# Attention weights of a windowed transformer block: the turn moved from TensorE products to 32x32 block transposes on VectorE, with all instruction orders replaced

## The chip, the cores and the metric

The kernel runs on one core of one Trainium2 chip. The metric is the device time of one execution in microseconds (us), from several runs; beside it there is one profiled execution, whose span (first to last instruction) and trace the text reads. TensorE is called PE below (PEld is its weight load), VectorE DVE, ScalarE ACT, GpSimd POOL, and SyncE SP. SP issues the transfers (DMAs).

## The reference

A transformer block with adaptive layer norm on 2048 tokens of width 512: attention over a dilated window, and a gated feed-forward network.

```python
# x: (1, 2048, 512), H = 32 heads of 16, W = 8 positions, dilation 2, F = 1792
mod = silu(c) @ w_mod                      # sa, ca, ga, sb, cb, gb
h = layernorm(x) * (1 + ca) + sa
q, k, v = h @ wqkv
idx = pos[:, None] - 2 * arange(8)         # token t sees t, t-2, ... t-14
logits = einsum('bhsd,bhswd->bhsw', q, k[idx]) * 16 ** -0.5
logits = where(idx >= 0, logits, -1e9)
attn = softmax(logits)
x = x + ga * (einsum('bhsw,bhswd->bhsd', attn, v[idx]) @ wo)
h = layernorm(x) * (1 + cb) + sb
x = x + gb * ((silu(h @ w1) * (h @ w3)) @ w2)
```

## The kernel before

**Tiles.** The tokens are 16 tiles of 128. Everything from the input x to the output of a tile stays in SBUF, but for v, which is stored to DRAM and read back with the window's shifts. Tiles are grouped differently in each stage: the first layer norm and the projections go by groups 0-1, 2-3, 4-7, 8-11, 12-15; logits, softmax and the weights' turn by pairs of tiles (eight pairs, each using one PSUM bank of 512 columns); the feed-forward network by the groups 0-1, 2-3, 4-7, 8-11, 12-13, 14-15.

**The attention of a tile.** `logits` (L731) multiplies q and the shifted keys on DVE, eight positions at once, into a tile `pq` of 128x4096 (`prod`, L742). There features lie on partitions. `red` (L752) sums over the 16 features of each head with TensorE: the PE array is used as four column groups of 32 (a "tiled" product), each group of 32 PSUM partitions takes a quarter of the tile's tokens, and its 32 partitions are the heads. So the PSUM bank holds, on partition (group, head), eight positions by 32 tokens for each of two tiles. For tile 0 a product of a constant `before` (made by POOL at the start, L395 to L397) adds the mask of positions ahead of the sequence (L749). `shift` takes the maximum over the positions (L764) and subtracts it (L769); `exps` is on ACT (L782); `softmax` sums (L794), takes the reciprocal (L796) and multiplies (L797), all on DVE, into `attn`, whose partitions are (group, head) and whose columns are (token, position).

**The turn.** The values need the weights with the tokens and positions on partitions: partition = position and token of a group of 16, columns = (one of eight token groups, head). `turn` makes that by four PE transposes a pair of tiles (L807) into a PSUM bank `ps_at`, which ACT copies to the SBUF tile `al` (L811).

**The values.** `values` (L815) loads a tile's shifted v with four transfers (L820), multiplies them with `al` on DVE (L827, 128x4096), sums over the positions on PE (`acc2`, L855, tiled), evicts on ACT (L861), turns the result with a transposing DMA, multiplies with wo on PE (L867) and adds to x on DVE (L871), which also yields the row sums of the second layer norm.

**Second layer norm and feed-forward.** `ln_sums` (L582): mean on POOL (L586), squares on ACT (L590), two further POOL steps (L596 and the next) and the bias (L599), normalization on ACT (L601). `ln_T` (L609) turns the result with transposing DMAs for the groups from 4-7 on and scales it on ACT (L621). `ffn_unit` (L876) does one of 14 units of 128 hidden features: w1 on PE, silu on ACT (L889), w3 on PE (both L883), product on DVE (L892). `ffn_w2` (L899) sums over the units (L921; L909 for the last two tiles), and `store` adds x on DVE (L931) and stores. Feed-forward units of earlier tiles run between the attention of later ones.

**What sets the order.** Each call of `p.op` records one operation of one engine (`p.dma` one transfer). `ORDER` (L980) is a list of all 1118 operations' numbers; each engine takes its own operations in that order, and within an engine nothing overtakes. `SLOTS` says which buffer or PSUM bank each value uses. `synchronize` (L165) then adds the semaphore waits. All transfers but one small one are issued by SP in the same list. The late weight parts (w1, w3 in four parts each, loads 14 to 21, and w2 in four, loads 22 to 25) have places in it like everything else.

## Time and profile before

| | |
|---|---|
| three runs | 239.23, 239.90, 240.03 us; median 239.9 |
| profiled execution, span | 237.7 us, TensorE clock 1.000 |
| PE busy | 229.7 us (97%) |
| DVE busy | 179.4 us (75%) |
| ACT busy | 138.5 us (58%) |
| POOL busy | 29.2 us (12%) |
| instructions | 4535 |

The page gives the span of the profiled execution and no time of its own beyond that; the median of the runs is 2.2 us above the span. Rows of the groups have the line, the engine, the operation, out<-in, shape and count, then the busy time and the mean of one record in ns, then the idle time of the engine just before, with what ended it. Rows of the timeline have the start, the duration, engine, line, operation and count; brackets hold a wait and what released it. Rows of the stretches have the window, its length, then for PE, PEld, DVE, ACT and POOL the busy us (and number of instructions), then the granted clock, the share of DMA and GB/s. Rows of the waits have the us waited, how often, and the longest.

### The profile page before, as it was taken

How to read it: one execution, taken by the hardware profiler on the slowest of the kernel's cores; microseconds unless marked ns; L12 is line 12 of the kernel's file. 1: busy time of each engine (PE TensorE's matmuls, PEld its weight loads, DVE VectorE, ACT ScalarE, POOL GpSimd, SP SyncE). 2: the span in 40 equal slices, each digit the busy share in tenths (PEclk: the TensorE clock that was granted, in tenths of full speed). 3: DMA queues.
4: the chain of work that ended last, by engine and by line, in shares of the span. 5: the costliest groups of instructions: out<-in, count | busy, mean ns of one | idle time of the engine just before them, and what ended most of it. 6: DMA issues, size and time to landing. Idle time of an engine off the chain costs nothing.

```text
span 237.7 us, 4535 instructions
## 1 busy us (share of the span) xinstructions
PE 229.7 (97%) x1781; PEld 136.2 (57%) x1806; DVE 179.4 (75%) x279; ACT 138.5 (58%) x267; POOL 29.2 (12%) x66
## 2 busy tenths in 40 slices
PE   7999999999999998999999999999999999999995
PEld 4776454445588674664444444444475457485774
DVE  5699999999999989999999999682654403434433
ACT  2289577999978744985865594837473405040300
POOL 4434100013002000240002520012010000000000
PEclk9999999999999999999999999999999999999999
DMA  6999999999999999897981693642203000000202
GB/s 216 372 337 322 158 237 299 208 269 283 353 200 270 243 249 199 173 260 177 247 234 47 182 234 72 154 132 46 67 19 91 3 0 0 6 19 0 70 0 88
DMA packets 46317, 38.85 MB, mean 163 GB/s; under 512 B 21704, under 2 KB 37080, under 8 KB 46296
## 3 DMA queue, kind: packets, MB, share of 16 engines
q1 hardware_dynamic: 46288, 38.56, 66.9%
q8 instruction: 14, 0.23, 0.4%
q14 instruction: 7, 0.06, 0.1%
q10 hardware_dynamic: 8, 0.00, 0.0%
HBM read 29.62 MB, written 4.21 MB: 142 GB/s over the span
## 4 chain that ended last, share of the span: by engine, by line
PE 74%; DMA 8%; DVE 8%; SPq 4%; ACT 3%; issue 2%; ACTq 0%; DVEq 0%
PE pall L883 38%; PE pall L921 18%; DMA sb_x<-in_A_x_dram 5%; PE pall L867 5%; SPq L124 4%; PE pall L691 4%; DMA sb_vsh<-v_scratch_dram 3%; PE pall L909 3%; PE pall L855 2%; PE pall L752 2%; PE pall L711 2%; DVE sb_vsh L827 2%; DVE sb_pq L742 2%; DVE sb_hh L892 1%; ACT sb_h L621 1%
## 5 line engine op out<-in xcount | busy, mean ns | idle before, releaser
L883 PE MATMUL pall<-sb_h,sb_w 128*128 128x256 bf16 (+1 forms) x664 | 101.9, 307 | 1.8 <-DVE sb_hh L892 0.9
L883 PEld LDWEIGHTS pall<-sb_h,sb_w 128*128 128x128 bf16 x672 | 64.8, 98 | 37.2 <-issue 2.8
L889 ACT ACTIVATE sb_sg<-pall 128x256 bf16<-128x256 f32 (+1 forms) x84 | 35.6, 453 | 54.1 <-PE pall L883 53.0
L892 DVE TENSOR_TENSOR sb_hh<-sb_sg,pall 128x256 bf16<-128x256 bf16 (+1 forms) x84 | 39.9, 505 | 34.8 <-PE pall L883 32.7
L921 PE MATMUL pall<-sb_w,sb_hh 128*128 128x512 bf16 x190 | 44.0, 379 | 0.3
L742 DVE TENSOR_TENSOR sb_pq<-sb_q,sb_kT 128x4096 bf16<-128x4096 bf16 x16 | 36.3, 2282 | 0.0
L921 PEld LDWEIGHTS pall<-sb_w,sb_hh 128*128 128x128 bf16 x196 | 19.0, 98 | 21.6 <-DVE sb_hh L892 0.4
L691 PE MATMUL pall<-sb_h,sb_wqkv 128*128 128x512 bf16 (+1 forms) x154 | 30.2, 335 | 0.5 <-issue 0.2
L827 DVE TENSOR_TENSOR sb_vsh<-sb_vsh,sb_al 128x4096 bf16<-128x4096 bf16 x12 | 27.3, 2287 | 2.1 <-DMA sb_vsh<-v_scratch_dram 2.1
L621 ACT ACTIVATE sb_h<-sb_h,sb_modc 128x512 bf16<-128x512 bf16 (+1 forms) x24 | 16.5, 743 | 10.1 <-DMA sb_h<-sb_xn 10.1
L691 PEld LDWEIGHTS pall<-sb_h,sb_wqkv 128*128 128x128 bf16 x160 | 14.7, 98 | 11.8 <-ACT sb_ac L861 0.4
L931 DVE TENSOR_TENSOR sb_o<-pall,sb_x 128x512 bf16<-128x512 f32 (+1 forms) x18 | 11.1, 625 | 10.5 <-PE pall L921 6.8
L711 PE MATMUL pall<-sb_wqkv,sb_h 128*128 128x512 bf16 x62 | 15.5, 379 | 0.2
L867 PE MATMUL pall<-sb_wo,sb_ot 128*128 128x512 bf16 x61 | 15.3, 379 | 0.3 <-issue 0.2
L586 POOL TENSOR_SCALAR sb_nm<-sb_sx 128x2 f32<-128x2 f32 x8 | 1.7, 218 | 105.2 <-DVE sb_x L871 105.1
L644 ACT ACTIVATE sb_h<-pall,sb_modc 128x256 bf16<-128x256 bf16 (+1 forms) x18 | 9.9, 612 | 7.5 <-DVE sb_modc L509 6.5
L861 ACT ACTIVATE sb_ac<-pall 128x512 bf16<-128x512 f32 x16 | 9.5, 595 | 7.2 <-PE pall L855 7.1
L601 ACT ACTIVATE sb_xn<-sb_x,sb_nb,sb_rs 128x512 bf16<-128x512 bf16 x16 | 12.4, 806 | 0.7 <-POOL sb_nb L599 0.6
L871 DVE SCALAR_TENSOR_TENSOR sb_x<-pall,sb_x 128x512 bf16<-128x512 f32 x16 | 10.9, 686 | 1.5 <-PE pall L867 1.3
L590 ACT ACTIVATE sb_xn<-sb_x,sb_nm 128x512 bf16<-128x512 bf16 x16 | 11.4, 714 | 0.7 <-POOL sb_nm L586 0.7
L721 ACT ACTIVATE sb_v<-pall 128x512 bf16<-128x512 f32 x16 | 9.5, 600 | 2.8 <-PE pall L711 2.8
L555 DVE BATCH_NORM_STATS2 sb_st<-sb_x 128x6 f32<-128x512 bf16 x16 | 10.6, 680 | 0.8 <-DMA sb_x<-in_A_x_dram 0.7
(87 smaller groups left out, 208.3 us busy)
## 6 DMA issues: line engine op xcount, KB each, us to landing
sb_vsh<-v_scratch_dram SPq DMA_DIRECT2D x48, 256.0 KB, 5.5
sb_vshx<-v_scratch_dram SPq DMA_DIRECT2D x16, 256.0 KB, 4.6
sb_w<-in_B_w_dram SPq DMA_DIRECT2D x6, 512.0 KB, 7.9
sb_w<-in_B_w_dram SPq DMA_DIRECT2D x6, 384.0 KB, 5.4
v_scratch_dram<-sb_v SPq DMA_DIRECT2D x16, 128.0 KB, 6.4
out_dram<-sb_o SPq DMA_DIRECT2D x14, 128.0 KB, 1.8
sb_wqkv<-in_A_wqkv_dram SPq DMA_DIRECT2D x6, 256.0 KB, 6.3
sb_x<-in_A_x_dram SPq DMA_DIRECT2D x4, 256.0 KB, 6.4
```

Of the source, the lines that this page charges most:

```text
L590: p.op("act", lambda e, vn=vn, T=T: e.activation(vn.at[:], x_sb[:, T, :], ACT.Square, bias=nm[:, T, :], accum_out=var[:, T, :]), c_act(512 ...
L601: p.op("act", lambda e, vn=vn, T=T: e.activation(vn.at[:], x_sb[:, T, :], ACT.Identity, bias=nb[:, T, :], scale=rs[:, NT + T, :]), c_act(5 ...
L621: return e.activation(vh.at[:, ft, 0:n * P], vh.at[:, ft, 0:n * P], ACT.Identity, bias=modc[:, 8 * which + ft:8 * which + ft + 1], scale=m ...
L691: ins = e.matmul(bank(vp)[:, j * n:(j + 1) * n], wqkv[:, t, col:col + P], vh.at[:, t, 0:n], start=(t == ORDER[0] and j == 0), stop=(t == O ...
L711: ins = e.matmul(bank(vp), vh.at[:, t, tt * P:(tt + 1) * P], wqkv[:, t, 2 * D:3 * D], start=(t == ORDER[0]), stop=(t == ORDER[-1]))
L742: return e.tensor_tensor(vp.at[:], in0, in1, ALU.mult)
L827: return e.tensor_tensor(v_w, v_w, a_w, ALU.mult)
L867: ins = e.matmul(bank(vy), vt.at[:, ft, :], wo[:, ft, :], start=(ft == 0), stop=(ft == KT - 1))
L883: ins = e.matmul(bank(vp)[:, 0:n], wt[:, t, fi * P:(fi + 1) * P], vh.at[:, t, 0:n], start=(t == 0), stop=(t == KT - 1))
L889: p.op("act", lambda e: e.activation(vt.at[:, 0:n], bank(vgp)[:, 0:n], ACT.Silu), c_act(n), k, r=[vgp], w=[vt], table="silu")
L892: p.op("dve", lambda e: e.tensor_tensor(vh_.at[:, 0:n], vt.at[:, 0:n], bank(vup)[:, 0:n], ALU.mult), c_dve(n), k, r=[vt, vup], w=[vh_])
L921: ins = e.matmul(bank(vz), vhh[fi].at[:, tt * P:(tt + 1) * P], w2[:, fi, :], start=(fi == 0), stop=(fi == NF - 1))
```

## The change

The change has three parts.

The turn: `attn` is turned by two DVE block transposes a pair of tiles, which transpose each 32x32 block by itself (32 partitions of one column group by 32 columns), straight into `al` in SBUF. The four PE transposes, the PSUM bank `ps_at` and the ACT copy are gone. Each of the two instructions takes 256 elements of every partition.

The tokens: a block transpose stays inside its 32 partitions. So that each lands where the values need it, column group q of `red` now takes tokens 8q to 8q+7 of every 32 (four runs of eight, where it took two interleaved rows of 16 from one 32). The mask of tile 0 then concerns two column groups in place of one; `before` is made by two selects and added by two products.

The orders: `ORDER` and `SLOTS` are replaced as a whole. There are 1111 operations: PE 376 (before 384), DVE 271 (263), ACT 233 (241), POOL 63 (62), SP 168 (168).

```diff
-    before = sb([P, W, 2, 16], bf, "before")
+    before = sb([P, 2, W, 4, 8], bf, "before")
...
-    p.op("pool", lambda e: e.affine_select(out=before[:], in_=before[:], compare_op=ALU.is_ge, fill=BEFORE, base=0,
-                                           pattern=[[-DIL, W], [1, 2], [2, 16]], channel_multiplier=0), 400, k, w=[vbefore])
+    for q in range(2):
+        p.op("pool", lambda e, q=q: e.affine_select(out=before[:, q], in_=before[:, q], compare_op=ALU.is_ge, fill=BEFORE, base=8 * q,
+                                                    pattern=[[-DIL, W], [32, 4], [1, 8]], channel_multiplier=0), 400, k, w=[vbefore])
...
                 if T == 0:
-                    e.matmul(PALL[0:32, c0:c0 + W * 32], ones[:, 0:32], before[:], start=True, stop=False, tile_position=(0, 0))
+                    for q in range(2):
+                        e.matmul(PALL[32 * q:32 * q + 32, c0:c0 + W * 32], ones[:, 0:32], before[:, q], start=True, stop=False,
+                                 tile_position=(0, 32 * q))
                 for ft in range(KT):
                     for q in range(4):
-                        ins = e.matmul(..., E_sb[:, ft, :], bass.AP(vp.at, ft * P + 32 * q, [[W * KT * P, P], [KT * P, W], [1, 2], [2, 16]]),
-                                       start=(ft == 0 and (T > 0 or q > 0)), ...)
+                        ins = e.matmul(..., E_sb[:, ft, :], bass.AP(vp.at, ft * P + 8 * q, [[W * KT * P, P], [KT * P, W], [32, 4], [1, 8]]),
+                                       start=(ft == 0 and (T > 0 or q > 1)), ...)
...
-        vt, val = Val("ps_at", psum), Val("al", alpool)
+        val = Val("al", alpool)
 
         def turn(e):
-            b = bank(vt).bitcast(bf)
-            for i in range(n):
-                at = b[:, i * 256:(i + 1) * 256].rearrange("p (q y h) -> p q y h", q=4, y=2)
-                for y in range(2):
-                    ins = e.transpose(at[:, :, y, :], bass.AP(ve.at[0], i * W * 32 + y * 16 * W, [[2 * W * 32, P], [1, P]]), ident[:])
+            for y in range(2):
+                at = bass.AP(ve.at[0], W * y, [[2 * W * 32, P], [64, 4 * n], [16, 4], [1, W]])
+                ins = e.transpose(bass.AP(val.at, H * y, [[2 * 8 * H, P], [2 * H, 4 * n], [1, H]]), at)
             return ins
 
-        p.op("pe", turn, 114 * n, ("at", Ts[0]), r=[va, vident], w=[vt], hold=[ve])
-        p.op("act", lambda e: e.activation(val.at[:, 0:n].rearrange("p n g h -> p (n g h)"), bank(vt).bitcast(bf)[:, 0:2 * n * P], ACT.Copy),
-             c_act(256 * n), ("at", Ts[0]), r=[vt], w=[val])
+        p.op("dve", turn, 120 + 267 * n, ("at", Ts[0]), r=[va], w=[val], hold=[ve], lead=o, lock=False)
         return val
...
 ORDER = [
-    8, 9, 10, 0, 20, 21, 22, 3, 4, 1, 2, 16, ...
+    18, 8, 9, 10, 0, 21, 22, 23, 3, 4, 1, 2, ...
 ]
 SLOTS = [
...
```

On the queues, what changes places: on SP the fourth part of w1 (load 20) goes from place 46 to place 20, ahead of the first stores of v, and the first part of w2 (load 22) from place 66 to place 45, ahead of the loads of shifted values of tiles 2 and 3. On DVE and PE the attention of the pairs and the feed-forward units between them come in another order throughout.

More of the change, by code (lines that the diff above doesn't have):

```diff
@@ L748, in red @@
                 if T == 0:
-                    e.matmul(PALL[0:32, c0:c0 + W * 32], ones[:, 0:32], before[:], start=True, stop=False, tile_position=(0, 0))
+                    for q in range(2):
+                        e.matmul(PALL[32 * q:32 * q + 32, c0:c0 + W * 32], ones[:, 0:32], before[:, q], start=True, stop=False,
+                                 tile_position=(0, 32 * q))
                 for ft in range(KT):
                     for q in range(4):
-                        ins = e.matmul(PALL[32 * q:32 * q + 32, c0:c0 + W * 32], E_sb[:, ft, :], bass.AP(vp.at, ft * P + 32 * q, [[W * KT * P, P], [KT * P, W], [1, 2], [2, 16]]),
-                                       start=(ft == 0 and (T > 0 or q > 0)), stop=(ft == KT - 1), tile_position=(0, 32 * q))
+                        ins = e.matmul(PALL[32 * q:32 * q + 32, c0:c0 + W * 32], E_sb[:, ft, :], bass.AP(vp.at, ft * P + 8 * q, [[W * KT * P, P], [KT * P, W], [32, 4], [1, 8]]),
+                                       start=(ft == 0 and (T > 0 or q > 1)), stop=(ft == KT - 1), tile_position=(0, 32 * q))
                 return ins
```

2 lines of the change are left out of this document (1 added, 1 removed), and 132 rows, old and new, of tables (ORDER, SLOTS).

## The prediction, made before the changed kernel was run

> **What bounds the kernel now.** I read the page first (span, busy time, slices), then the busy time in stretches of 10 us, then the waits, and last the timeline around the places where TensorE came late.
>
> ```profile
> span 237.7 us, 4535 instructions
> PE 229.7 (97%) x1781; PEld 136.2 (57%) x1806; DVE 179.4 (75%) x279; ACT 138.5 (58%) x267; POOL 29.2 (12%) x66
> PE   7999999999999998999999999999999999999995
> DVE  5699999999999989999999999682654403434433
> DMA  6999999999999999897981693642203000000202
> ```
> ```profile
> 80.00:90.00 10.00, 9.13 (x99) 6.44 (x88) 8.82 (x9) 4.31 (x11) 0.00 (x0) 1.00 1.17 239
> 110.00:120.00 10.00, 9.84 (x89) 4.83 (x89) 9.90 (x10) 8.32 (x12) 0.00 (x0) 1.00 1.03 247
> 190.00:200.00 10.00, 9.95 (x67) 6.39 (x66) 1.77 (x4) 2.88 (x8) 0.00 (x0) 1.00 0.00 0
> ```
> ```profile
> PE pall L883 <- DVE sb_hh L892: 0.9, 1, 0.9
> DVE sb_vsh L827 <- DMA sb_vsh<-v_scratch_dram: 2.1, 3, 1.0
> ```
>
> TensorE (PE) is busy in nearly every slice, so its work sets the end. But up to about 155 us VectorE (DVE) is just as full: 9.90 of 10 us in the stretch from 110, while ScalarE has room. After that DVE falls to 1.77 of 10 and PE alone counts. DMA is full up to about 95 us. So the first 155 us have two limits side by side. PE work taken away there is worth its time only if DVE does not come later by more than the room between them. That PE is not wholly free of DVE shows in the waits: its one long wait, 0.9 us, was for a DVE product.
>
> **The change, part by part.**
>
> ```profile
> L807 PE MATMUL pall<-sb_ident,sb_attn 128*128 128x128 bf16 x32 | 3.1, 219 | 0.0
> L811 ACT ACTIVATE sb_al<-pall 128x512 bf16<-128x512 bf16 x8 | 4.8, 598 | 1.5 <-PE pall L807 1.3
> L749 PE MATMUL pall<-sb_before,sb_ones 128*32 128x256 bf16 x1 | 0.3, 283 | 0.0
> L396 POOL TENSOR_SCALAR_AFFINE_SELECT sb_before<-sb_before 128x256 bf16<-128x256 bf16 x1 | 0.5, 530 | 0.1
> L892 DVE TENSOR_TENSOR sb_hh<-sb_sg,pall 128x256 bf16<-128x256 bf16 x56 | 21.8, 417 | 25.2 <-PE pall L883 24.9
> L794 DVE TENSOR_REDUCE sb_ssum<-pall 128x64 f32<-128x512 f32 x8 | 5.5, 683 | 0.0
> L796 DVE RECIPROCAL sb_ssum<-sb_ssum 128x64 f32<-128x64 f32 x8 | 4.4, 551 | 0.2
> L576 DVE TENSOR_SCALAR sb_xn<-sb_x,sb_mv,sb_rs 128x512 bf16<-128x512 bf16 x15 | 5.5, 398 | 1.5 <-POOL sb_rs L565 1.5
> ```
> ```profile
> 35.22 0.22 PE pall L807 x4
> ...
> 111.06 0.55 PE pall L855 x8
> ```
>
> *Removed from PE.* 32 transposes, four to a pair of tiles. Their records last 219 ns, but matmuls overlap: on the chain four take 0.22 us. Eight groups of 0.22 are 1.76 us off the engine that sets the end. *Added to PE.* The mask of tile 0 is two products in place of one. They lie on different column groups, so between 0 and 0.28 us (the L749 row); I take 0.1. The other products change only the order in which they read their moving operand; the forms and counts stay. No row shows a dearer reading order, so I take 0.
>
> *Removed from ACT.* Eight evictions of 0.60, 4.8 us. ACT is 58% busy, so I cost that at nothing; where it may have counted, ahead of tile 15's multiplication, the stage is past the place that decides below. *POOL.* One 0.53 us select becomes two over half the width: at least 0, at most 0.53 us more. It stands in POOL's idle first microseconds; if that cover were gone it would be 0.5 us at the start.
>
> *Added to DVE.* Sixteen block transposes of 256 bf16 elements, two to a pair of tiles. Here the overlap of records has to be taken off:
>
> ```profile
> 60.31 2.29 DVE L827 TENSOR_TENSOR sb_vsh<-sb_vsh,sb_al 128x4096 bf16<-128x4096 bf16 x1 [0.26 <-DMA sb_vsh<-v_scratch_dram]
> ...
> 87.14 2.29 DVE L827 TENSOR_TENSOR sb_vsh<-sb_vsh,sb_al 128x4096 bf16<-128x4096 bf16 x1 [1.04 <-DMA sb_vsh<-v_scratch_dram]
> 89.36 1.40 DVE L892 TENSOR_TENSOR sb_hh<-sb_sg,pall 128x256 bf16<-128x256 bf16 x4
> 90.75 2.29 DVE L827 TENSOR_TENSOR sb_vsh<-sb_vsh,sb_al 128x4096 bf16<-128x4096 bf16 x1
> ...
> 99.57 0.68 DVE L797 TENSOR_TENSOR sb_attn<-pall,sb_ssum 128x512 bf16<-128x512 f32 x1
> 100.17 0.74 DVE L892 TENSOR_TENSOR sb_hh<-sb_sg,pall 128x256 bf16<-128x256 bf16 x2
> ```
>
> Four products of 256 elements run from 89.36 to 90.75, so one moves DVE on by 0.35 us though its record lasts 0.42; one of 512 elements moves it on by 0.60 (99.57 to 100.17). The trace has no block transpose. From below: L576 handles 512 bf16 in a 0.40 us record, so a fast form of 256 might take 0.20. From above: two cycles an element would be the 512 price, 0.60. I take 0.35, the row with the same number of elements: 16 x 0.35 = 5.6 us of DVE, 2.8 of it ahead of tile 6.
>
> The Trainium skill has a price for this (VectorE: DVE Perf Modes, The three transpose paths): 311 ns for 128x128 bf16 on VectorE against 390 ns on TensorE. Our piece is two such blocks wide; as an estimate by that page its record is at most 0.62 us, 0.2 above the L892 record, and the sum below would come out up to 1.6 us later (eight pieces), on the side of rival B. The TensorE figure does not fit here: the rows have 219 ns a record and 0.22 us for four.
>
> *The orders.* What matters is how far each engine must work before the places where one waits for the other, so I counted the instructions of both lists up to each such place. One place decides. The two tightest:
>
> ```profile
> 98.95 0.69 DVE L871 SCALAR_TENSOR_TENSOR sb_x<-pall,sb_x 128x512 bf16<-128x512 f32 x1
> ...
> 100.83 2.28 DVE L742 TENSOR_TENSOR sb_pq<-sb_q,sb_kT 128x4096 bf16<-128x4096 bf16 x1
> 101.65 1.52 POOL L596 TENSOR_SCALAR sb_rs<-sb_var 128x2 f32<-128x2 f32 x1 [0.70 <-ACT sb_xn L590]
> ...
> 109.17 2.93 ACT L621 ACTIVATE sb_h<-sb_h,sb_modc 128x512 bf16<-128x512 bf16 x4 [2.99 <-DMA sb_h<-sb_xn]
> 112.84 0.76 PEld L883 LDWEIGHTS pall<-sb_h,sb_w 128*128 128x128 bf16 x5 [0.43 <-ACT sb_ac L861]
> ```
> ```profile
> 107.49 2.28 DVE L827 TENSOR_TENSOR sb_vshx<-sb_vshx,sb_al 128x4096 bf16<-128x4096 bf16 x1
> ...
> 110.99 0.62 PE L855 MATMUL pall<-sb_vshx,sb_ind 128*32 128x512 bf16 x8
> ```
>
> Place 1, the start of the feed-forward group of tiles 4 to 7. It needs the last residual (tile 6, L871, ends 99.64), from there POOL, ACT, four transposing DMAs and the four L621, which end at 109.17 + 2.93 = 112.10: a chain of 12.5 us. PE loads its first weights of the group at 112.84, so there is room of 0.74 us. In the new order DVE has ahead of that residual four pairs of turns (8 x 0.35 = 2.8) and four products (1.4) more, one sum (0.60), one reciprocal (0.55) and one output addition (0.60) less: +2.45. PE has ahead of the group's first matmul five groups of transposes less (1.1) and one accumulation less (0.55): -1.65. The two draw apart by 4.1 us against a room of 0.74: PE would wait 3.36 us.
>
> From that come off the DVE waits that need not recur once DVE runs later: the data of tiles 7 and 2, for which it waited 1.04 and 0.26, have that much longer to land. That leaves 2.06 us. Bounds: no wait goes, 3.36; and beyond those two, DVE's cheapest turn saves 8 x 0.15 = 1.2, so 0.86. The chain itself I leave at 12.5. The 1.52 us of POOL's L596 end at 103.17, right after the long product of DVE (100.83 to 103.11), while others of POOL take a fifth of that: POOL was held. In the new order tile 10's product follows the residual by 2.8 us, and holds a later POOL step instead.
>
> Place 2, tile 9's accumulation: multiplication ends at 109.77, PE starts at 110.99, room 1.2. DVE gets five pairs (3.5) and loses one addition (0.6); PE loses five groups of transposes and gets two reductions, together about 0. So 2.9 - 1.2 - 1.3 = 0.4 us of waiting. It lies just ahead of place 1 and is part of the 2.06, not added to it. Later there is more room than before: ahead of tile 14's accumulation PE has 8.5 us more (ten half units of feed-forward, two second products, less the rest) and DVE 6.4.
>
> *Transfers.* All on SP's queue. The fourth part of w1 moves ahead of the first stores of v, and the first part of w2 ahead of the shifted values of tiles 2 and 3.
>
> ```profile
> sb_w<-in_B_w_dram SPq DMA_DIRECT2D x6, 512.0 KB, 7.9
> ...
> 52.65 7.64 DMA sb_vsh<-v_scratch_dram
> ```
>
> The values of tile 2 are on the chain: issued at 52.65, landed 60.29, when DVE took them at 60.31. A 512 KB part ahead of them is 2.2 us of traffic at the 239 GB/s of the row for 80 to 90 us. DVE multiplies tile 2 ahead of tile 3 now (before: 3, then 2), and the turn itself delays it by two pieces, 0.7 us. I take 0 and keep 0 to 1.5 us (2.2 less 0.7) for the range. By tile 7 the same ten weight parts are ahead in both orders.
>
> *Sum.* -1.76 + 0.1 + 2.06 = +0.4 us on the span: 238.1. The profile gives a span of 237.7 and no time around it; the median of the runs, 239.9, lies 2.2 above. I leave those 2.2 as they are: 240.3 us. Of this kernel's time 0.3% are 0.72 us, about what a measurement can tell from no change.
>
> **The rivals.**
>
> A, PE's gain stands: 239.9 - 1.66 = 238.2. It needs the 2.06 us to vanish. For it: PE is the busiest engine, DVE's other waits in the stage may go too, and the turn may run in a fast form (0.20 each: wait 0.86, time 239.1). Against it: DVE has no idle time left between 100 and 150, and the counts are what they are. Between 238.2 and 239.1.
>
> B, slower, by the price of the turn alone. Eight pieces lie ahead of place 1, so each 0.1 us on a piece is 0.8 us there. From 0.39 us on (0.04 x 8 = 0.32 on top of 0.4) the result is slower than before by 0.72; at 0.60 it is 0.4 + 2.0 = 2.4, 242.3. For it: the input is read in runs of eight elements from four places, and no row shows what the block form costs to fill and drain; besides, a pair's first piece reads what L797 has just written and can't overlap it (0.68 less 0.60, 0.08 a pair, 0.3 us for four). Against: L892 also writes and reads two operands at one element a cycle.
>
> C, slower, by the w2 part ahead of the values of tiles 2 and 3: DVE waits up to 1.5 us at tile 3 and hands it on, since it has no idle time to absorb it: 241 to 241.8.
>
> D, the change doesn't do what it says: the turn needs more than two instructions to a pair. Then the price is B's, and it is counted there.
>
> **How the numbers follow.** Main case 0.40, its own range 239.6 to 241.2 (the wait from 1.4 to 3.0); A 0.25; B 0.20; C 0.15. Faster: A nearly whole and a little of main, 0.26. Within 0.3% (239.2 to 240.6): three quarters of main, and the edges of the others, 0.38. Slower: the rest of main, most of B and C, 0.36. The range 238.3 to 242.3 leaves out the lower end of A and prices above 0.60.
>
> **What would show it.** No L807 and L811 groups; DVE transposes x16 with a record near 0.42 us. PE's wait list gets a wait of about 2 us at L883 between 110 and 115 us, released by ACT L621, and the wait for L892 at about 88 us goes. The chain of waits passes through L871, the POOL steps, the transposing DMA and L621. If A is right, there is no such wait and PE is busy 9.8 of 10 in every stretch; if B, the record is 0.5 us or more; if C, DVE waits for sb_vsh near 60 us. The prediction is wrong if PE waits at a place that I hold to have room, above all after 120 us, or if the chain from the residual to L621 is much shorter or longer than 12.5 us.

## The result, and the profile after

The changed kernel takes 245.77 us (median of four runs, 244.81 to 246.90) against 239.73 before (239.23 to 240.03): a ratio of 1.0272, 95% interval 1.0224 to 1.0319. It is 6 us slower; I had forecast 240.3. (The kernel before ran once more for this comparison, hence four runs.) The profiled execution spans 243.6 us (its time is 245.37), against 237.7. A few executions show a lower granted clock and take some per cent longer; the ratios are formed without them.

The page of the changed kernel, its first lines, one slice row and the row of the turn:

```profile
span 243.6 us, 4496 instructions
PE 231.7 (95%) x1775; PEld 134.9 (55%) x1775; DVE 183.2 (75%) x295; ACT 134.8 (55%) x259; POOL 28.4 (12%) x67
PE   6999999889999799889799999999999999999995
...
L808 DVE STREAM_TRANSPOSE sb_al<-sb_attn 128x256 bf16<-128x256 bf16 x16 | 6.1, 422 | 0.0
```

The turn costs what was forecast: 16 records of 422 ns. PE's busy sums can't be compared (231.7 here, 229.7 before): the trace of before has 1781 products for 1806 weight loads, so 25 records are missing there. PE's row has slices of 7 and 8 tenths where it had 9. The waits of PE say for what (columns: us in all, how often, the longest):

```profile
PE pall L866 <- DMA sb_ot<-sb_ac: 3.2, 3, 1.6
PE pall L882 <- ACT sb_h L622: 1.8, 2, 1.3
PE pall L920 <- DVE sb_w L951: 1.3, 1, 1.3
```

L866 is the product with wo (L867 before): PE waits for the transposing DMA of the attention output. L882 is the feed-forward product (L883 before), L920 the one with w2. There are no transposes and copies of the turn any more, and the wait for L892 near 88 us is gone. Where these waits come from is seen on DVE and along the chain to place 1, in the timeline:

```profile
42.28 0.58 SPq L124 DMA_DIRECT2D sb_w<-in_B_w_dram  x1
43.45 2.75 SPq L124 DMA_TRANSPOSE sb_ot<-sb_ac  x2
...
49.69 1.90 PE L866 MATMUL pall<-sb_wo,sb_ot 128*128 128x512 bf16 x8 [1.65 <-DMA sb_ot<-sb_ac]
50.76 0.69 DVE L870 SCALAR_TENSOR_TENSOR sb_x<-pall,sb_x 128x512 bf16<-128x512 f32 x1 [1.11 <-PE pall L866]
...
71.64 0.59 SPq L124 DMA_DIRECT2D sb_w<-in_B_w_dram  x1
79.09 1.23 DVE L951 TENSOR_TENSOR sb_w<-sb_w,sb_gb_bc 128x2048 bf16<-128x2048 bf16 x1 [2.19 <-DMA sb_w<-in_B_w_dram]
...
93.86 0.58 SPq L124 DMA_DIRECT2D sb_w<-in_B_w_dram  x1
95.49 2.28 DVE L826 TENSOR_TENSOR sb_vsh<-sb_vsh,sb_al 128x4096 bf16<-128x4096 bf16 x1
95.61 0.61 SPq L124 DMA_DIRECT2D sb_w<-in_B_w_dram  x1
...
99.58 1.21 SPq L124 DMA_TRANSPOSE sb_ot<-sb_ac  x1
104.26 1.04 PE L866 MATMUL pall<-sb_wo,sb_ot 128*128 128x512 bf16 x4 [1.08 <-DMA sb_ot<-sb_ac]
105.34 0.69 DVE L870 SCALAR_TENSOR_TENSOR sb_x<-pall,sb_x 128x512 bf16<-128x512 f32 x1 [1.53 <-PE pall L866]
...
115.41 2.93 ACT L622 ACTIVATE sb_h<-sb_h,sb_modc 128x512 bf16<-128x512 bf16 x4 [2.96 <-DMA sb_h<-sb_xn]
118.39 3.84 PE L882 MATMUL pall<-sb_h,sb_w 128*128 128x512 bf16 x17 [1.30 <-ACT sb_h L622]
```

The issues of weight parts (sb_w) are SP's: the second part of w2 at 71.64, the two last at 93.86 and 95.61, ahead of the transposing DMA of tile 6 at 99.58. The product of tile 6's values (95.49, ends 97.77) ended at 90.75 + 2.29 = 93.04 before. Tile 6's residual (L870, ends 106.03) ended at 99.64. The input of the feed-forward group of tiles 4 to 7 is ready at 115.41 + 2.93 = 118.34, where it was at 112.10: 6.24 us later, and the span is 5.9 longer. So place 1 sets the end, as forecast, and the question is why it comes 6 us later and not 2. For comparison, the same transfers, scaling and product in the trace of before:

```profile
55.21 1.16 SPq L124 DMA_DIRECT2D sb_w<-in_B_w_dram  x2
67.97 1.22 DVE L952 TENSOR_TENSOR sb_w<-sb_w,sb_gb_bc 128x2048 bf16<-128x2048 bf16 x1
...
87.70 1.11 SPq L124 DMA_DIRECT2D sb_w<-in_B_w_dram  x2
92.09 3.57 SPq L124 DMA_TRANSPOSE sb_ot<-sb_ac  x2
97.88 1.04 PE L867 MATMUL pall<-sb_wo,sb_ot 128*128 128x512 bf16 x4
```

The first row issues a part of w3 and the second part of w2, the second row scales that part, without a wait. The third row issues the two last parts; the second transposing DMA of the fourth is tile 6's, issued at 94.47. The busy time of the engines from 20 us to the end of tile 6's product, in the trace of before and then of after (window, its length, then PE, PEld, DVE, ACT, POOL):

```profile
20.00:93.04 73.04, 71.07 (x659) 42.75 (x665) 70.77 (x90) 57.18 (x113) 6.75 (x13) 1.00 1.15 257
```
```profile
20.00:97.77 77.77, 73.61 (x647) 43.72 (x646) 72.77 (x100) 57.01 (x113) 8.60 (x14) 1.00 0.98 243
```

DVE has 2.00 us more work (72.77 - 70.77) and stands idle 5.00 us in place of 2.27. Work +2.00, waits +2.73: that is the +4.73 of this product. (Counted from the start of the span it is +1.51 and +3.22, because this execution also began later; see *What stays open*.) Another 1.66 lies between product and residual (8.26 us for 6.60), above all in the transposing DMA: from its issue to PE's product 4.68 us (99.58 to 104.26), before 3.41 (94.47 to 97.88). From the residual on nothing is lost (12.31 us to the input, 12.46 before), nor from the input to the end (243.6 - 118.34 = 125.3; 125.6 before). So the span's 5.9 are settled by 106 us.

### The profile page after: what moved, and what is told of

It reads as the page before. It is cut to its first block, busy times and chain, and to the rows that moved or that the text cites. A ratio compares the mean times of both kernels' runs of the same rounds, so it can differ in the third digit from the quotient of the medians.

```text
span 243.6 us, 4496 instructions
## 1 busy us (share of the span) xinstructions
PE 231.7 (95%) x1775; PEld 134.9 (55%) x1775; DVE 183.2 (75%) x295; ACT 134.8 (55%) x259; POOL 28.4 (12%) x67
## 4 chain that ended last, share of the span: by engine, by line
PE 44%; ACT 5%; DMA 2%; SPq 1%; POOL 1%; DVE 0%; issue 0%
PE pall L882 29%; PE pall L920 7%; PE pall L866 3%; PE pall L908 3%; ACT sb_h L622 2%; DMA sb_h<-sb_xn 2%; PE pall L854 1%; SPq L124 1%; ACT sb_xn L602 1%; ACT sb_xn L591 1%; ACT L785 1%; ACT pall L785 0%; PE pall L755 0%; POOL sb_rs L598 0%; DVE sb_x L870 0%
## 5 line engine op out<-in xcount | busy, mean ns | idle before, releaser
L882 PE MATMUL pall<-sb_h,sb_w 128*128 128x256 bf16 (+1 forms) x672 | 102.1, 308 | 2.2 <-ACT sb_h L622 1.8
L882 PEld LDWEIGHTS pall<-sb_h,sb_w 128*128 128x128 bf16 x672 | 64.7, 98 | 39.4 <-ACT sb_h L622 2.8
L920 PE MATMUL pall<-sb_w,sb_hh 128*128 128x512 bf16 x196 | 44.3, 379 | 1.3 <-DVE sb_w L951 1.3
L920 PEld LDWEIGHTS pall<-sb_w,sb_hh 128*128 128x128 bf16 x196 | 19.0, 98 | 22.8 <-DVE sb_w L951 1.6
L826 DVE TENSOR_TENSOR sb_vsh<-sb_vsh,sb_al 128x4096 bf16<-128x4096 bf16 x13 | 29.5, 2285 | 0.9 <-DMA sb_vsh<-v_scratch_dram 0.8
L692 PEld LDWEIGHTS pall<-sb_h,sb_wqkv 128*128 128x128 bf16 x160 | 15.2, 98 | 13.1 <-ACT sb_h L645 0.6
L866 PE MATMUL pall<-sb_wo,sb_ot 128*128 128x512 bf16 x64 | 16.0, 379 | 3.2 <-DMA sb_ot<-sb_ac 3.2
L870 DVE SCALAR_TENSOR_TENSOR sb_x<-pall,sb_x 128x512 bf16<-128x512 f32 x16 | 10.9, 689 | 9.2 <-PE pall L866 9.1
L587 POOL TENSOR_SCALAR sb_nm<-sb_sx 128x2 f32<-128x2 f32 x8 | 2.4, 297 | 130.8 <-DVE sb_x L870 130.7
L712 PE MATMUL pall<-sb_wqkv,sb_h 128*128 128x512 bf16 x64 | 16.8, 379 | 0.0
L866 PEld LDWEIGHTS pall<-sb_wo,sb_ot 128*128 128x128 bf16 x64 | 5.8, 97 | 11.3 <-DMA sb_ot<-sb_ac 3.5
```

Source lines behind the costliest of these rows:

```text
L692: ins = e.matmul(bank(vp)[:, j * n:(j + 1) * n], wqkv[:, t, col:col + P], vh.at[:, t, 0:n], start=(t == ORDER[0] and j == 0), stop=(t == O ...
L712: ins = e.matmul(bank(vp), vh.at[:, t, tt * P:(tt + 1) * P], wqkv[:, t, 2 * D:3 * D], start=(t == ORDER[0]), stop=(t == ORDER[-1]))
L826: return e.tensor_tensor(v_w, v_w, a_w, ALU.mult)
L866: ins = e.matmul(bank(vy), vt.at[:, ft, :], wo[:, ft, :], start=(ft == 0), stop=(ft == KT - 1))
L882: ins = e.matmul(bank(vp)[:, 0:n], wt[:, t, fi * P:(fi + 1) * P], vh.at[:, t, 0:n], start=(t == 0), stop=(t == KT - 1))
L920: ins = e.matmul(bank(vz), vhh[fi].at[:, tt * P:(tt + 1) * P], w2[:, fi, :], start=(fi == 0), stop=(fi == NF - 1))
```

## The experiments

Fourteen kernels ran, each timed beside the kernel before. "After" is the changed kernel. The theories stand in the expectations as they were at that run: T1, the new orders and the places of the weight parts carry the loss; T2, the turn's own time on DVE does; T3, a wait of DVE or PE for a transfer is handed on to the end; T4, PE has run out of other work ahead of place 1, so that a wait that is removed comes back at the next place. Ratios are to the kernel before on the same chip, and kernels are compared by them.

**1. The turn alone, in the orders of before.**

```diff
 DVE order:  ... product of the softmax, ...
+            turn(pair)          # where the PE turn stood in the list
 PE order:
-            turn(pair)
 ACT order:
-            copy ps_at -> al
```

> The changed turn and token deal alone, in the orders of before: the block transposes stand where the list of before has the PE transposes, the ACT copies are left out of it, everything else keeps its place. Theory T1 (the loss of 6 us comes from the new orders, above all from the places of the weight parts among the transfers): the turn itself costs little; four pairs ahead of tile 6's residual make DVE up to 2.8 us later there, PE is 0.9 us shorter, the room is 0.74 and DVE's waits for shifted values absorb up to 1.3: a wait of PE of 1 to 3 us ahead of the feed-forward group of tiles 4 to 7, less 1.8 us of transposes: 239 to 241.5 us. Theory T2 (the loss is DVE's added 5.6 us of turns): 243 us or more.

Measured: 242.46 us, ratio 1.0131 (1.0070 to 1.0192). Between the two theories and nearer T1: the turn by itself, with the new deal of tokens, makes the kernel slower, by about half of the loss (between a quarter and seven tenths of it by the interval). In the trace it does it without a wait at place 1:

```profile
20.00:93.53 73.53, 71.96 (x656) 41.78 (x653) 73.18 (x101) 56.03 (x110) 5.66 (x15) 1.00 1.14 257
```
```profile
PE pall L854 <- DVE sb_vsh L826: 1.7, 4, 0.7
PE pall L854 <- DVE sb_hh L891: 0.8, 1, 0.8
PE pall L920 <- DVE sb_hh L891: 0.5, 1, 0.5
```

Here DVE's waits did go, as I had assumed for the changed kernel: 2.27 us of idle time became 0.35, so 2.41 us of work made tile 6's product only 0.49 us later. PE pays in small pieces where it needs a product that DVE has just made (L854, L920), 3.0 us in these rows; its waits of this kind were 1.5 us before (0.9, 0.4 and 0.2).

**2. The new orders alone, with PE transposes and ACT copies.**

```diff
 after's lists, with
-  DVE turn(pair)
+  PE  turn(pair)
+  ACT copy ps_at -> al
```

> The new orders alone: kernel of before (PE transposes, ACT copy, old token deal) in the orders of after, the PE transposes and the copy at the place where after has the block transposes, their PSUM bank taken where one is free. T1: PE has its 1.8 us of transposes again and the waits for transfers stay: 245 to 248 us. T2: DVE is 6 us shorter and PE's waits go: 240 to 242 us.

Measured: 256.51 us, ratio 1.0703 (1.0652 to 1.0754), outside both. The wait list of this run says why: DVE's products of the values wait for the copy.

```profile
DVE sb_vsh L827 <- ACT sb_al L811: 21.1, 6, 6.2
PE pall L855 <- DVE sb_vsh L827: 9.9, 3, 5.2
```

The new lists give the weights no time on PE and in ACT's queue. That they need the short turn is shown; how good they are with it is not, so this run does not tell T1 from T2.

**3. The last two parts of w2 earlier, in after.**

```diff
 SP order:   ... vshx loads (tile 7) x3
+            w2_2, w2_3
             loads of tiles 6, 7; ot 5, ot 4
-            w2_2
             v 13, load of tile 9
-            w2_3
             ot 7, ..., ot 6
```

> The changed kernel with one edit: the last two parts of w2 are issued 12 and 14 us earlier, in SP's idle stretch from 78.3 us, and no longer just ahead of the transposing transfers of tiles 7 and 6. T1: PE's waits for those at 101 and 103 us (0.5 and 1.1) go, the residual of tile 6 comes 1.5 us earlier and with it the chain to the group of tiles 4 to 7, whose wait (1.3) shrinks: 242.5 to 244.3 us. T2: no change, 245.8 within 0.7.

Measured: 246.04 us, ratio 1.0284 (1.0235 to 1.0333): no change, T1 missed. One of the two waits at 101 to 103 us went. The other stayed (1.09 us): with no part of w2 near it in the queue the transposing DMA of tile 6 still took 4.01 us to PE's product. The second part of w2 landed later and PE's wait for it was 2.4 us in place of 1.3; and ahead of every transfer that was moved DVE had already stood 1.95 us for the values of tiles 0 and 1, against 0.55 in after. The profiled execution was the slowest of the four, so this trace doesn't settle what the edit is worth.

**4. All badly placed parts moved at once.**

```diff
 SP order:
-            w2_0, w1_0 ahead of ot 0, ot 1
             ot 0, ot 1
+            w1_0
             ... w1_2, w3_0, w3_2, w3_1
+            w2_0, w2_1
             ot 2, ...                      (w2_2, w2_3 as in 3)
```

> The changed kernel with all the weight parts that stand badly moved: as in the run before, and the first and second part of w2 in SP's idle stretch from 60.5 us, and the first part of w1 behind the transposing transfers of tiles 0 and 1 rather than ahead of them. T1: the waits at 48 us (1.65), 79 us (1.3), 101 and 103 us (1.6) and a part of that at 117 us (1.3) go: 239.5 to 241.5 us. T2: 244.5 us or more, PE waiting for DVE in their place.

Measured: 247.21 us, ratio 1.0309 (1.0252 to 1.0366): T1 missed again. The time is in T2's range, and PE did wait for DVE, but DVE stood idle: it is a wait of my own making. DVE comes to the scaling of w2_0 at 65 us, and now it had not landed:

```profile
69.77 1.23 DVE L951 TENSOR_TENSOR sb_w<-sb_w,sb_gb_bc 128x2048 bf16<-128x2048 bf16 x1 [4.27 <-DMA sb_w<-in_B_w_dram]
...
74.18 1.04 PE L866 MATMUL pall<-sb_wo,sb_ot 128*128 128x512 bf16 x4 [3.88 <-DVE sb_hh L891]
```

DVE stands 4.27 us at a weight that nobody needs yet, and PE 3.88 us for a feed-forward product behind it in DVE's queue. The first part of w1 made another: it now stands ahead of the values of tiles 2 and 3, and DVE waits 2.36 us for them (0.28 in after). Two things are to be seen beside that. With the weight parts behind ot 0 and ot 1, PE's first product with wo started at 48.09 without a wait, where after has 1.65 us. And behind PE's long wait the granted clock fell (the column behind POOL's, here 0.67), which makes this loss larger than the wait:

```profile
74.00:78.00 4.00, 3.82 (x14) 1.78 (x15) 3.63 (x10) 3.80 (x6) 0.00 (x0) 0.67 1.07 246
```

**5. After with the turn all but left out.**

```diff
-            for y in range(2):
-                ... e.transpose(..., at)            # 256 columns each
+            return e.transpose(al[:, one block], attn[:, one block])   # 32 columns
```

> The changed kernel with the turn all but left out: one block transpose of 32 columns a pair in place of two of 256, the weights for the values being a constant set at the start (so this leaves out the turn of the weights). DVE is 5 us shorter, the orders are those of after. Theory T2 (DVE's added time makes the loss): 239 to 241 us. Theory T1, narrowed by the runs before (the larger part lies in the new orders, whose waits for transfers are there whatever DVE does): 242.5 to 244.5 us, with the wait for w2 near 79 us and that for the turned values near 48 us still there.

Measured: 246.46 us, ratio 1.0286 (1.0222 to 1.0351). T2 falls: in these orders the turn's time, taken away, brings nothing that can be measured; and T1's figure was still 2 us too low. The stretch to tile 6's product, then two rows of the timeline:

```profile
20.00:97.32 77.32, 74.14 (x649) 43.81 (x648) 71.02 (x97) 57.44 (x114) 8.60 (x14) 1.00 1.01 245
```
```profile
79.21 1.23 DVE L953 TENSOR_TENSOR sb_w<-sb_w,sb_gb_bc 128x2048 bf16<-128x2048 bf16 x1 [1.87 <-DMA sb_w<-in_B_w_dram]
...
99.13 1.21 SPq L124 DMA_TRANSPOSE sb_ot<-sb_ac  x1
104.25 1.04 PE L868 MATMUL pall<-sb_wo,sb_ot 128*128 128x512 bf16 x4 [2.21 <-DMA sb_ot<-sb_ac]
```

DVE's work falls from 72.77 to 71.02, but its idle time rises from 5.00 to 6.30: both kernels meet at the landing of the second part of w2 (79.09 and 79.21). What is left, 0.45 us at tile 6's product, goes at the next transfer: the transposing DMA is issued 0.45 earlier (99.13 for 99.58), and PE gets it at 104.25 for 104.26. A gain on an engine that then waits for a transfer is no gain. (Setting the constant costs something at the start: PE's longer row of first products began at 3.94 us, 3.62 in after, and the first projection at 9.33, 9.00 in after.)

**6. After with the turn done twice.**

```diff
+            for t in (al_twice, al):        # the first buffer is read by nobody
                 for y in range(2): e.transpose(t, ...)
```

> The changed kernel with every block transpose done twice (the first time into a buffer that nobody reads): DVE 5.6 us longer again, nothing else changed. T2: most of the 5.6 us shows: 249.5 to 251.5 us. T1: DVE has room in these orders while PE waits for transfers: 246 to 249 us.

Measured: 248.41 us, ratio 1.0374 (1.0317 to 1.0430), inside T1's range, though not for T1's reason, that DVE has room: 1.0 per cent, 2.4 us, more than after, for 2.7 us of DVE ahead of place 1 (8 pieces of about 0.34) and as much behind it. DVE has 75.14 us of work to the end of tile 6's product, 2.37 more than after, and 4.93 of idle time:

```profile
20.00:100.07 80.07, 74.32 (x650) 44.04 (x648) 75.14 (x107) 57.27 (x113) 8.60 (x14) 1.00 0.97 235
```

In these traces DVE's time ahead of place 1 counts nearly in full when it is added (tile 6's product 2.30 us later), and hardly when it is taken away (5, 0.45 earlier). The times of the runs alone, with their intervals, would not show that difference.

**7. The orders of before, with the turn all but left out.**

```diff
 the lists of 1, and
-                ... e.transpose(..., at)            # two of 256 columns
+            return e.transpose(al[:, one block], attn[:, one block])   # 32 columns
```

> The turn in the orders of before, all but left out as in the first of these runs (one block transpose of 32 columns a pair, constant weights). PE has lost 1.8 us of transposes, ACT its copies, DVE gets next to nothing. If DVE's lateness is what costs in the run with the turn alone (242.5), PE's gain stands here: 237 to 238.5 us. If it is the new deal of tokens or something else: 240 us or more.

Measured: 239.65 us, ratio 1.0054 (1.0022 to 1.0087): in microseconds between the two ranges, by the ratio (241.0 on the scale of the 239.73 above) in the second, and still slower than before. PE has lost its 1.8 us, DVE has almost nothing to do for it, and the gain is not there. In the trace the start took 1.1 us (the first projection at 9.30 us, 8.19 before; the constants add memsets to DVE there), and at the next feed-forward group, tiles 8 to 11, PE stands for its input, as it did not before:

```profile
153.14 1.04 PE L884 MATMUL pall<-sb_h,sb_w 128*128 128x512 bf16 x4 [1.31 <-ACT sb_h L627]
```

The new order in which PE reads its operand is not the cause: its records of the sums last 274 ns (272 before).

**8. The turn in the orders of before, with room made.**

```diff
 PE order:
+            q 14                ahead of the sums of tiles 0, 1   (from behind them)
+            v 12                ahead of the sum of tile 3
+            z(tile 0, first half) ahead of the sum of tile 5
+            f 29                between the sums of tiles 11 and 10
 DVE order:
+            turn(8, 9)          behind three feed-forward products
```

> The turn in the orders of before, with five moves to give PE work where it waited for DVE in the run with the turn alone: one projection product ahead of the sums of tile 1, one ahead of those of tile 3, the first half of tile 0's last product ahead of those of tile 5, one half unit between tile 11's sum and what follows, and the turn of pair 8-9 behind three feed-forward products on DVE. If those waits (0.3, 0.7, 0.4, 0.8, 0.5) are the cost: 239 to 240.5 us. If DVE's lateness only shows at the next place: 241.5 to 243 us.

Measured: 243.88 us, ratio 1.0189 (1.0140 to 1.0238). The second answer, 0.9 us above its range: the products pulled forward waited in their turn, for a PSUM bank that ACT had not yet emptied (0.8 and 0.7 us) and for the next group's input (1.1).

**9. Only the second part of w2 earlier, in after.**

```diff
 SP order:   w3_1
+            w2_1
             ot 2, w3_3, ot 3, v 12, three loads of tile 5
-            w2_1
```

> The changed kernel with one edit: the second part of w2 is issued 11 us earlier, in SP's idle stretch from 60.5 us. In after it lands at 79.1, DVE stands 2.2 us at its scaling with everything behind it, and PE 1.3 us. Theory T3 (weight parts that DVE must scale stand late among the transfers and hold DVE's queue, and by it the chain to the residual of tile 6; with the turn left out that chain was only 0.45 us earlier, since both runs met at this landing): PE's wait near 79 goes, and of those at 101 to 117 us (2.9) a part: 242 to 244.3 us. Rival T4 (the list as a whole is tight, and each wait taken away comes back at the next place): 245 to 246.5 us.

Measured: 245.36 us, ratio 1.0256 (1.0232 to 1.0281): T4's range. DVE's wait of 2.19 and PE's of 1.3 near 79 us are gone, and the input of the group of tiles 4 to 7 still comes at 118.57 (118.34 in after), because tile 6's residual came no earlier. Its transposing DMA was issued at 99.03, 0.55 before after's, and PE got it at 104.49:

```profile
99.03 1.21 SPq L124 DMA_TRANSPOSE sb_ot<-sb_ac  x1
104.49 1.04 PE L866 MATMUL pall<-sb_wo,sb_ot 128*128 128x512 bf16 x4 [1.90 <-DMA sb_ot<-sb_ac]
```

That is 5.46 us, 0.78 more than in after, with the two last parts of w2 ahead of it as there. The start hides a part of the gain: the first projection began at 9.54 us, 9.00 in after.

**10. Three moves: 9, 3, and the first part of w2 behind ot 0 and ot 1.**

```diff
 SP order:
-            w2_0 ahead of ot 0, ot 1
             w1_0, ot 0, ot 1
+            w2_0                (ahead of loads of the values of tiles 2, 3)
             ... w3_1
+            w2_1                (as in 9)
             ... vshx loads (tile 7)
+            w2_2, w2_3          (as in 3)
```

> As in the run before, and the first part of w2 behind the transposing transfers of tiles 0 and 1 (not 4 us ahead of them; DVE scales it 18 us later), and the third and fourth part in SP's idle stretch from 78.3 us. T3: the waits at 48 us (1.65) and 79 us go, and a part of those at 101 to 117: 240.5 to 243 us. T4: 244.5 us or more.

Measured: 243.85 us, ratio 1.0194 (1.0165 to 1.0224): 1.9 us less than after, just past T3's range on T4's side. The group's input comes 1.4 us earlier (114.01 + 2.93 = 116.94).

```profile
61.22 4.49 DVE L826 TENSOR_TENSOR sb_vsh<-sb_vsh,sb_al 128x4096 bf16<-128x4096 bf16 x2 [1.85 <-DMA sb_vsh<-v_scratch_dram]
...
99.43 1.20 SPq L124 DMA_TRANSPOSE sb_ot<-sb_ac  x1
102.86 1.04 PE L866 MATMUL pall<-sb_wo,sb_ot 128*128 128x512 bf16 x4 [0.51 <-DMA sb_ot<-sb_ac]
...
114.01 2.93 ACT L622 ACTIVATE sb_h<-sb_h,sb_modc 128x512 bf16<-128x512 bf16 x4 [2.97 <-DMA sb_h<-sb_xn]
```

The first row is rival C, made by my move: w2_0 now stands right ahead of the values of tiles 2 and 3, and DVE waits 1.85 us for them, so tile 6's product is no earlier than in after (97.63 for 97.77). The gain is the next two rows: the transposing DMA, issued as late as in after (99.43 for 99.58), is there after 3.43 us and not 4.68, now that no part of w2 is issued just ahead of it.

**11. The three moves, with the turn all but left out.**

```diff
 the lists of 10, and
-                ... e.transpose(..., at)            # two of 256 columns
+            return e.transpose(al[:, one block], attn[:, one block])   # 32 columns
```

> The three moves of the run before, with the turn all but left out (one block transpose of 32 columns a pair, constant weights). If the transfers hid what the turn costs, DVE's 5 us show here: 2 us or more below the run before. If the turn costs nothing in these orders: within 1 us of it.

Measured: 243.06 us, ratio 1.0167 (1.0131 to 1.0203): 0.3 per cent below 10, with overlapping intervals. The four runs lie far apart (241.24, 242.41, 243.72, 252.48); the median of the lower three is 1.4 us below that of 10. The profiled execution has more of it: tile 6's product ends at 94.76, 2.87 us earlier than in 10, the group's input comes at 114.10 (116.94), and the span is 239.5 (242.1); it was the shortest of that kernel's runs.

```profile
20.00:94.76 74.76, 73.70 (x647) 43.82 (x646) 70.74 (x97) 57.32 (x114) 9.71 (x14) 1.00 1.02 258
```

DVE's idle time is 4.02 us here and 4.71 in 10 (77.63 - 72.92 to its tile 6 product). By the runs the turn is worth 0.7 to 1.4 us in these orders, by the two traces 2.6: the two expectations are not told apart.

**12. The kernel of before, its first part of w2 issued later.**

```diff
 SP order:   w2_1, v 7
-            w2_0
             ot 3, w3_3, w1_2, ot 2, w3_2, four loads of tile 5
+            w2_0
```

> The kernel of before with one edit: the first part of w2 is issued behind the four loads of tile 5's shifted values, 4 to 7 us later, so that it lands after DVE comes to its scaling at 74.3 us, as the second part does in after. T3: DVE stands there for 2 to 4 us and PE behind it: 1.5 to 4 us more than before. T4: no change within 0.7 us, DVE and PE having room.

Measured: 245.48 us, ratio 1.0266 (1.0236 to 1.0296): T3's way, and above its range. One transfer moved, no other instruction touched, and the loss is as large as that of the whole change. Rows of the timeline, and a stretch:

```profile
79.13 1.23 DVE L952 TENSOR_TENSOR sb_w<-sb_w,sb_gb_bc 128x2048 bf16<-128x2048 bf16 x1 [4.69 <-DMA sb_w<-in_B_w_dram]
80.75 1.89 PE L883 MATMUL pall<-sb_h,sb_w 128*128 128x256 bf16 x8 [4.37 <-DVE sb_hh L892]
...
115.99 2.93 ACT L621 ACTIVATE sb_h<-sb_h,sb_modc 128x512 bf16<-128x512 bf16 x4 [2.95 <-DMA sb_h<-sb_xn]
```
```profile
79.00:83.00 4.00, 2.25 (x10) 1.48 (x11) 3.73 (x8) 0.92 (x2) 0.00 (x0) 0.50 1.06 278
```

DVE stands 4.69 us, tile 6's product ends at 98.72 (93.04 before), the group's input is ready at 115.99 + 2.93 = 118.92 (112.10). The wait alone doesn't explain 6.4 us: PE stood for 4.37 us, and then the granted clock was 0.50 until about 85 us. So this run shows that such a wait reaches the end, but not at what rate; after, whose clock is 1.000 throughout, has no such addition.

**13. Experiments 9 and 3 together, the first part of w2 left where after has it.**

```diff
 SP order:   ... w3_1
+            w2_1                (as in 9)
             ... vshx loads (tile 7)
+            w2_2, w2_3          (as in 3)
```

> After, with experiments 9 and 3 together: the second part of w2 behind w3_1, the last two parts ahead of the loads of tiles 6 and 7; the first part stays where after has it, ahead of the values of tiles 2 and 3. T3 (the waits of DVE and PE for transfers ahead of place 1 add up, and each comes off the end when it goes): the 2.19 us of DVE at 79 us go, and the second transposing DMA of tile 6 takes about 3.4 us from issue to its product as in 10 (4.68 in after), 1.25 us less. The input of the group of tiles 4 to 7 comes at 118.34 - 2.19 - 1.25 = 114.9, the time is 242.3, ratio 1.010 to 1.015. T4 (a wait removed comes back at the next place): input at 116.5 or later, ratio 1.018 or more.

Measured: 243.00 us, ratio 1.0152 (1.0091 to 1.0214): 1.2 per cent, 2.9 us, less than after. That is just past T3's range, and nearer to it than to T4's; the interval holds both. The input of the group decides for T3. The stretch, and rows of the timeline:

```profile
20.00:96.16 76.16, 73.23 (x646) 43.66 (x644) 72.43 (x98) 56.85 (x113) 8.96 (x14) 1.00 1.04 253
```
```profile
51.25 0.69 DVE L870 SCALAR_TENSOR_TENSOR sb_x<-pall,sb_x 128x512 bf16<-128x512 f32 x1 [1.27 <-PE pall L866]
...
97.98 2.20 SPq L124 DMA_TRANSPOSE sb_ot<-sb_ac  x1
101.36 1.04 PE L866 MATMUL pall<-sb_wo,sb_ot 128*128 128x512 bf16 x4 [0.46 <-DMA sb_ot<-sb_ac]
...
112.50 2.93 ACT L622 ACTIVATE sb_h<-sb_h,sb_modc 128x512 bf16<-128x512 bf16 x4 [2.96 <-DMA sb_h<-sb_xn]
```

The wait at 79 us is gone (DVE's idle time 3.73 for 5.00), the transposing DMA takes 3.38 us (97.98 to 101.36) for 4.68, and the input comes at 115.43: 2.91 us earlier than in after, 0.5 later than I had worked out. PE's wait at place 1 is 1.30 as in after, since PE came earlier too. Of the 2.91, 0.7 may be its start (the first projection at 8.28 us, 9.00 in after). So the two waits come off together, though neither did alone (3, 9). That the second stood behind the first fits this, but the traces of 3 and 9 have other waits and starts as well (see there), so the size of each is not shown. The wait of 1.27 us at 51 us is still there; its part of w2 was not moved.

**14. The two moves, with the turn all but left out.**

```diff
 the lists of 13, and
-                ... e.transpose(..., at)            # two of 256 columns
+            return e.transpose(al[:, one block], attn[:, one block])   # 32 columns
```

> As 13, with the turn all but left out (32 of 512 columns, so the weights that enter the values are not all turned). T3: with no transfer in the way the eight pieces ahead of place 1 cost their 0.34 us each: input 2.5 to 3 us earlier than in 13, ratio 0.010 to 0.013 lower, that is 1.000 to 1.004. T4: input at most 1.5 us earlier than in 13, ratio less than 0.006 lower.

Measured: 242.79 us, ratio 1.0127 (1.0062 to 1.0191), 0.0025 below 13 with overlapping intervals: T4's side. So once more the turn's 2.7 us ahead of place 1 are worth little when they are taken out of the new orders: 0.6 us here; as an estimate from the spread of the runs (242.54 to 243.47 in 13, 242.05 to 243.14 for three of the four here) at most about 1.5. The trace is not used: the profiled execution was the longest of the four (247.19 us).

## Why the prediction was wrong

**The step that failed** is "From that come off the DVE waits that need not recur". I subtracted 1.3 us for two waits of before. The larger did go (1.04, tile 7), the smaller stayed (0.26 became 0.28, now for tiles 2 and 3), and new ones came: 0.55 at 38.43 for the values of tiles 0 and 1, 1.11 at 50.76, 0.61 at 69 and 2.19 at 79.09. DVE's idle time ahead of tile 6's product rose by 2.73 where I let it fall by 1.3. That is 4.0 us of the 5.5 by which I was low. I had asked only which waits need not recur, and not which the new order makes.

**Behind it lies the transfers' paragraph.** I named two moved parts of weights and found that neither hurts, on one comparison: the values of tiles 2 and 3. That comparison was right; DVE waits 0.28 there, and C did not happen. But the new list moves other parts too, and the second part of w2 (load 23) later: from place 64 to 75 on SP, behind the transposing DMAs of tiles 2 and 3. Each part should have been set against its own first user, and against the short transfers behind it in SP's queue. Before, the second part of w2 was issued by 56.4 us and DVE scaled it at 67.97, and the first at 58.57 and 74.29, both without a wait; in after the second is issued at 71.64, DVE is ready for it at 76.9, and it lands at 79.1. The two last parts stand ahead of the transposing DMA of tile 6, which reached PE 1.25 us sooner in 10 and 13, where they don't. They stood ahead of it before too, but further: the last was issued about 6 us before it then, and 4.0 in after. And w2_0 and w1_0 stand ahead of those of tiles 0 and 1 (1.65 us of PE; 1.28 in 10 with w1_0 alone ahead, none in 4 with neither). In my sum these were 0. Experiment 13 gives 2.9 us back by moving three of them.

**Terms, one by one.** PE's transposes: -1.76 forecast, and PE has none left; what that saves can't be read from the busy sums (see the result). POOL: I had two selects over half the width and 0 to 0.53 us; they have the old width, 1.3 us for 0.53, and the fill ahead of them takes 0.52 for 0.31, so 1.0 us more. In after PE's first products behind them begin 0.16 us later (3.62 for 3.46 us); whether by that is not shown. From span to time I added 2.2; in the four executions of after it is 1.7 to 1.8, so the forecast was 0.4 too high by this term. The turn: 0.42 us a record as taken from L892, and two pieces in a row take 0.76; right, so B's price is not the cause. As an estimate from the 311 ns of the Trainium skill (VectorE: DVE Perf Modes, The three transpose paths) a record could have lasted up to 0.62; the trace's 0.42 decides. DVE's work ahead of place 1: +2.45 forecast, +2.15 measured from 20 us to tile 6's residual (78.69 for 76.54). The chain from the residual to the group's input: 12.5 forecast, 12.31 measured, and a later step of POOL falls beside the long product of DVE (108.55 to 110.83) and is held, as forecast; for the other pair of the group the same step took 0.19 us:

```profile
109.03 1.86 POOL L600 TENSOR_TENSOR sb_nb<-sb_nm,sb_rs 128x2 f32<-128x2 f32 x1
```

The chain from product to residual, which I did not look at: +1.66. PE's wait at place 1: 2.06 forecast, 1.30 measured, because PE had waited 1.65, 1.34, 0.52 and 1.08 us on the way and came late as well. That place 1 decides was right; that its price is the wait seen there was not. The price is how late the input comes, since from there to the end before, after and 13 take the same 125.3 to 125.6 us.

**Rivals.** A fell, and not by the turn's price alone: with the turn all but left out in the orders of before (7) nothing was gained. In that trace the 1.8 us taken from PE are matched by a start 1.1 us later and a new wait of 1.3 at the next group. B named the wrong price but not the wrong engine: the turn alone in the old orders costs 1.3 per cent (1). C did not occur in after; I made waits of its kind myself in 4 and 10. I gave 0.36 to slower, and the range ended 2.5 us below the lowest run.

**What stays open.** How the loss divides between turn and orders has no single answer here: the turn alone costs 3.1 us in the old orders, 2.4 more when doubled in the new ones, and between nothing and 1.4 by the runs when left out of them (5, 11, 14), where setting the constant costs a few tenths. In 13 about 3.6 us of loss remain, more than half; a wait at 51 us and DVE's 1.66 us of added work are in its trace, and 14 speaks against the turn as most of it. What the rest is, no run shows. Part of the difference between single executions is the start: the first projection began at 8.19 us before, 9.00 in after, 8.28 in 13, with 17 of the 24 first PE products at the slow 0.42 us before and all 24 in after. It differs between executions with the same orders too (8.28 in 3, 9.54 in 9), so these 0.8 us are in part chance. No version that I ran beats the kernel before.

## What to carry to other kernels

When orders change, list every load with its first user in the new order and with the short transfers that it now precedes; the waits that a change makes are not in the profile of before, and must be looked for in the lists. Where two engines are both full, a microsecond taken from one of them is worth what the next wait, here most often for a transfer, leaves of it, while a microsecond added was paid nearly in full (6). And two waits in a row can hide each other: here moving one showed nothing (3, 9), and both together 2.9 us (13).

## What the runs showed that I had not expected

A transposing DMA of 128x512 bf16 whose data is ready late seems to depend still on what was issued ahead of it. For tile 6's it was 3.4 to 3.5 us from issue to PE's product with no weights near it in the queue (4, 10, 11, 13), but 4.0 in 3, which has the same queue there. It was 4.7 to 5.5 us with two parts of w2 issued 5.7 and 4.0 us earlier (after, 5, 6, 9), but 3.4 in before, 1 and 7 and 4.3 in 8, where the later of the two was issued 5 to 6 us earlier. So not the place in the queue alone counts; that the distance does is not tested.

The granted clock fell after long waits of PE: 3.88 us in experiment 4 and 4.37 in 12 were followed by some us at 0.50, while waits up to 1.65 us in after left it at 1.000. The Trainium skill (TensorE: Matmul & The Clock Gate, Why this matters for your kernels) advises to keep PE's gaps under about 3 us for that reason; these two waits agree. For shorter ones the length alone does not decide: 2.42 us in 3 left the clock at 1.000, and in 5, where PE waited 2.21 us and was busy for 2.05 of the 4 us from 100 on, it fell to 0.50 from 106 to 108. So a wait that seems to cost 4 us can cost more.
